# One matmul for V's mean row, one normalisation per head, and third-product operands made a quarter earlier

## The chip, the cores and the metric

The kernel runs on one core of a Trainium2 chip. The metric is the device time of one execution in microseconds (us); a lower time is better. Names of engines as the profile has them: PE is the matrix engine (PEld its weight loads), DVE the vector engine, ACT the scalar engine, POOL the GpSimd engine, SP the engine that issues most DMA transfers (SPq is its queue of issues).

## What is computed

Three stages follow each other, all in fp32 at the interface:

```python
mask   = q_bucket[:, :, :, None] == k_bucket[:, :, None, :]   # 6 sign bits of q@proj, k@proj
scores = np.where(mask, q @ k.T / 8, -1e9)                    # B=2, H=8, S=768, D=64
attn   = softmax(scores) @ v                                  # 16 heads
x = attn -> (1536, 512)
h = max(x @ w1, x @ w2, x @ w3)                               # 512 -> 768
x = h @ w_out                                                 # 768 -> 512, "the third product"
h = x @ w_in                                                  # 512 -> 2048
out = (h * clip(h + 3, 0, 6) / 6) @ w_out2                    # 2048 -> 512
```

A query that shares its bucket with no key gets -1e9 everywhere, so its softmax is uniform and its output is the mean of V's rows.

## The kernel before

Precision is kept by splitting: an fp32 operand is written as a high part and a residual, and a product becomes three matmuls (high x high, high x residual, residual x high). The two large products after the third one are computed by a seven-product scheme on 2x2 blocks, whose operands are blocks (B11, B21, B22) and differences of blocks (T1 to T4), each split in two.

**Attention** (`attention()`, L357) is one list of 96 steps, s = (head h, half hf, block i). The order of work is written out by hand: functions are put on steps by `at` (before the steps' end) and `po` (the `late` tasks), with the offsets of tables such as `VA, VS, VC, VH` counted from a pair's first step s0 = 12p. The loop at the end of `attention()` issues, for each step s: the PV block of step s - LAG (LAG = 6); the tasks called `first` (the normalisation, and from step RAMP = 8 on every task whose name isn't in AFTER); the scores of step s; the row maxima of a later head (`max_unit`); the split of the exponentials of step s - 1; the remaining tasks; the late tasks; and pieces of weight preparation (`tick`). The engines' queues run in this order, each its own.

What the functions put on the engines:

- `scores` (L659 ff.): PE, four matmuls of 384 columns (L664) into two PSUM tiles "s"; ACT then takes the exponential (L668, tile E) and its fp16 copy (L671, ph); POOL (L686) or DVE makes the residual pl.
- `max_unit` (L609): PE, two matmuls (L614) into PSUM tiles "m" (three exist), each read out by a DVE maximum (L618).
- `pv` (L689): PE, 18 fp16 matmuls of 65 columns (L698 to L700) into the PSUM tile "x", of which there is one, and two matmuls (L703, L704) that add V's mean row to flagged queries. Their weights are the flag row FL (zero but in row 0), their moving operand is VM, whose row 0 holds the mean's high part and then its residual.
- `norm` (L706): DVE reads x: denominator (L710, xd), reciprocal (L715, xr), product (L718, xo), three blocks at a time, so twice per head.
- `fin` (L723): PE transposes xo (L726).
- `vsum` (L541): PE, one matmul with one column (L543) that reduces V's row maxima into an "m" tile; `vscale` (L545) is four small DVE steps on it (L549, L554 and on).
- `vmean` (L590): V's mean. `max_out` (L646): SP issues the transfers of the maxima's rows and of FL (L651).

**The third product** runs in four quarters (b, dh) = (0,0), (0,1), (1,1), (1,0), each with two column tiles d and six steps f of six matmuls (L1453). After each f the loop advances the generator `making` by MK = 0, 3, 3 or 2 steps (one step is one instruction) and prepares weights (`tick2`, by the table TQ). `making` is `xops` (L1150): for each block an optional subtraction on DVE (L1161, xF), the high part on ACT (L1164, xh) and the residual on DVE (L1166, xl) or POOL. At a quarter's end ACT evicts the PSUM tiles into xF (L1481). In the fourth quarter `seven` (L1197) begins between the f steps: its first product (L1210) is copied by ACT into c (L1216), and further products, c matmuls of L1210, are added on it. Weight preparation uses the names wy, wr, wh, wl, G (ACT L954, L956, L1015; DVE L961; POOL L984).

The lines of the third product's loop:

```python
for _ in range(MK[3 * b + dh - 2 * b * dh]):
    next(making, None)
tick2(TQ[3 * b + dh - 2 * b * dh][d % 2][f])
...
if (b, dh) == (0, 1):
    for _ in making:
        pass
    making = xops(0, [(free.pop(0), free.pop(0)) for _ in range(7)], XO[0])
```

The functions that the diff touches, and those that call them:

## Time and profile before

| | |
|---|---|
| median of 3 runs | 688.95 us (688.47 to 689.98) |
| the profiled execution's own time | 690.18 us |
| its span (first to last instruction) | 688.4 us |
| mean granted TensorE clock | 0.993 of 2.4 GHz |
| PE busy | 666.0 us, 97% of the span |
| DVE, ACT, POOL busy | 511.0, 432.8, 334.3 us |

The profile is of one execution; the times are of others, of the same program. A busy time is the sum over instructions; an idle time is given with the releaser, the instruction whose end allowed the engine to go on. Attention takes about the first 250 us, the first products of the next stage follow, the third product lies at about 373 to 438 us, and the large products fill the rest.

### The profile page before, as it was taken

Reading aid. Unit: us, or ns where it says so; the run is one execution under the profiler, and the core shown is the slowest. Engines: PE = TensorE matmul, PEld = TensorE weight load, DVE = VectorE, ACT = ScalarE, POOL = GpSimd, SP = SyncE. Lnnn points to the kernel's source line nnn. Section 1 sums busy time; section 2 is a strip of 40 time slices with the busy share of each in tenths; the row PEclk is TensorE's granted clock in tenths of the full one; section 3 lists DMA queues with packets and bytes.
Section 4 is the critical chain, followed back from the end, with each engine's and each line's share of the span. In section 5 each row is a group of like instructions: output and inputs, shape, how many; then the busy total and the mean of one; then the engine's idle time right before and its main releaser. Section 6 shows DMA issues by size and latency. Waiting matters only on the chain.

```text
span 688.4 us, 13482 instructions
## 1 busy us (share of the span) xinstructions
PE 666.0 (97%) x5189; PEld 613.2 (89%) x5189; DVE 511.0 (74%) x978; ACT 432.8 (63%) x749; POOL 334.3 (49%) x280
## 2 busy tenths in 40 slices
PE   8999999999999999999999996999999999999997
PEld 7789898888898989999999996989989889889986
DVE  6888988989985647677668477773868687877664
ACT  6667788889887525574746556676556565655520
POOL 6778898999987330654443543112142331313100
PEclk9999999999999999999999998999999999999999
DMA  6665557767441000211223222010203020211004
GB/s 191 170 153 136 160 123 184 191 167 190 103 90 63 2 1 32 92 62 62 62 92 120 96 64 89 31 62 1 92 30 123 31 92 31 92 61 62 1 0 184
DMA packets 22527, 61.80 MB, mean 90 GB/s; under 512 B 3864, under 2 KB 4952, under 8 KB 22464
## 3 DMA queue, kind: packets, MB, share of 16 engines
q1 hardware_dynamic: 22032, 60.55, 30.7%
q8 instruction: 41, 0.67, 0.4%
q10 hardware_dynamic: 432, 0.40, 0.2%
q14 instruction: 22, 0.18, 0.1%
HBM read 38.87 MB, written 3.15 MB: 61 GB/s over the span
## 4 chain that ended last, share of the span: by engine, by line
PE 63%; DVE 6%; ACT 2%; issue 1%; POOLq 0%; DVEq 0%; ACTq 0%
PE c L1210 16%; PE m L1210 11%; PE x L1536 10%; PE m L1536 9%; PE c L147 4%; PE m L307 3%; PE m L1453 2%; PE s L664 2%; PE c L1453 2%; PE x L1210 1%; DVE xF L1161 1%; PE x L698 1%; PE x L699 1%; PE x L700 1%; DVE mx L618 1%
## 5 line engine op out<-in xcount | busy, mean ns | idle before, releaser
L686 POOL TENSOR_TENSOR pl<-E,ph 128x768 f16<-128x768 f32 x85 | 152.4, 1808 | 30.4 <-ACT ph L671 17.2
L618 DVE TENSOR_REDUCE mx<-m 128x1 f32<-128x384 f32 x192 | 96.6, 546 | 12.3 <-PE m L614 11.4
L668 ACT ACTIVATE E<-s 128x768 f32<-128x768 f32 x96 | 78.1, 813 | 39.1 <-PE s L664 31.4
L671 ACT ACTIVATE ph<-s 128x768 f16<-128x768 f32 x85 | 68.9, 810 | 0.0
L698 PEld LDWEIGHTS <-ph 128*128 128x128 f16 x576 | 53.9, 98 | 16.3 <-issue 10.2
L698 PE MATMUL x<-VV,ph 128*128 128x65 f16 x576 | 64.5, 195 | 2.8 <-DVE xo L718 1.9
L699 PE MATMUL x<-VV,ph 128*128 128x65 f16 x576 | 64.1, 196 | 0.0
L700 PE MATMUL x<-VV,pl 128*128 128x65 f16 x576 | 63.7, 193 | 0.0
L614 PE MATMUL m<-T,T 76*128 76x384 f32 x192 | 54.0, 352 | 3.5 <-DVE mx L618 1.5
L664 PE MATMUL s<-QB,KB 128*128 128x384 f32 x192 | 56.7, 376 | 0.4 <-ACT ph L671 0.4
L699 PEld LDWEIGHTS <-ph 128*128 128x128 f16 x576 | 54.5, 98 | 0.7 <-issue 0.6
L700 PEld LDWEIGHTS <-pl 128*128 128x128 f16 x576 | 54.7, 99 | 0.0
L664 PE MATMUL s<-T,T 98*128 98x384 f32 x192 | 49.7, 340 | 0.3 <-DMA T<-mr 0.2
L1006 POOL TENSOR_TENSOR hF<-hF 128x256 f32<-128x256 f32 x8 | 6.6, 819 | 76.6 <-DVE hF L965 76.6
L614 PEld LDWEIGHTS m<-T,T 76*128 76x128 f32 x192 | 35.0, 188 | 9.6 <-DVE mx L618 5.7
L961 DVE SCALAR_TENSOR_TENSOR wy<-wy,wr 128x512 int32<-128x512 int32 x32 | 23.0, 718 | 25.9 <-ACT wr L956 25.9
L1554 DVE TENSOR_TENSOR xF<-x,xF 128x512 f32<-128x512 f32 (+1 forms) x43 | 29.4, 684 | 11.6 <-PE x L1536 11.5
L984 POOL TENSOR_TENSOR wl<-wy,wh 128x512 fp32r<-128x512 f32 x10 | 13.2, 1323 | 50.8 <-ACT wh L982 50.8
L1094 POOL TENSOR_TENSOR hF<-hF 128x256 f32<-128x256 f32 x6 | 6.5, 1090 | 62.7 <-DVE hF L1048 62.7
L664 PEld LDWEIGHTS s<-T,T 98*128 98x128 f32 x192 | 34.9, 189 | 0.9 <-DMA T<-mr 0.9
L984 POOL TENSOR_TENSOR wol<-wy,woh 128x512 fp32r<-128x512 f32 x6 | 8.0, 1342 | 51.6 <-ACT woh L982 51.6
L1252 ACT ACTIVATE gr<-m,half 128x384 f32<-128x384 f32 x30 | 17.4, 579 | 24.1 <-DVE m L1230 13.5
(472 smaller groups left out, 2198.2 us busy)
## 6 DMA issues: line engine op xcount, KB each, us to landing
wraw<-in_wts_dram SPq DMA_DIRECT2D x56, 512.0 KB
xF<-in_vP_dram SPq DMA_DIRECT2D x8, 384.0 KB
KB<-kH SPq DMA_DIRECT2D x15, 192.0 KB
QB<-qL SPq DMA_DIRECT2D x15, 192.0 KB
T<-kH SPq DMA_DIRECT2D x15, 192.0 KB
T<-qH SPq DMA_DIRECT2D x15, 192.0 KB
KB<-kL SPq DMA_DIRECT2D x15, 192.0 KB
QB<-qH SPq DMA_DIRECT2D x15, 192.0 KB
```

The lines of the kernel that those rows point to most:

```text
L614: pe.matmul(u[:, 0:HF], QA[h % NA][0:76, qt * 128:qt * 128 + 128], KA[h % NA][0:76, hsl(hf)], start=True, stop=True,)
L618: dve.tensor_reduce(out=mx[h][:, qt, hf:hf + 1], in_=u[:, 0:HF], axis=AX.X, op=ALU.max)
L664: pe.matmul(u[:, k, 0:HF], a[0:n, c], b[0:n, hsl(hf)], start=n == 128, stop=n < 128)
L668: act.activation(out=e, in_=u[:, :, 0:HF], func=AF.Exp, scale=BIG)
L671: act.activation(out=ph.rearrange("p (a b) -> p a b", a=2), in_=u[:, :, 0:HF], func=AF.Exp, scale=BIG,)
L686: eng.tensor_tensor(out=pl, in0=e, in1=ph, op=ALU.subtract)
L698: pe.matmul(o, ph[:, c], vv[:, 0:65], start=kt == 0, stop=False)
L699: pe.matmul(o, ph[:, c], vv[:, 65:130], start=False, stop=False)
L700: pe.matmul(o, pl[:, c], vv[:, 0:65], start=False, stop=False)
L1210: pe.matmul(u, l[:, s], r[i], start=first and i + j == 0, stop=i == 1 and j == 2, skip_group_check=not first,)
L1536: pe.matmul(u[:, 0:c1 - c0], (h, l, h)[k], (oh, oh, ol)[k][:, c0:c1], start=j == k == 0, stop=j == 1 and k == 2,)
L1554: dve.tensor_tensor(out=o, in0=u[:, 0:c1 - c0], in1=o, op=ALU.add)
```

## The change

- V's mean: `VM` is now one row of 65 columns per head, with the high part in row 0 and the residual in row 32 (of a tile that is cleared otherwise); the flag row is sent to rows 0 and 32 of FL, and one matmul adds both.
- All six PV blocks of a head go into one "x" tile, and `norm` is called once per head, on six blocks. Since there is one such tile, the first PV block of the next head is issued behind the scores and maxima of its step instead of ahead of them.
- V's scale matmul and the four DVE steps behind it move a step later (VS, VC), and with `vsum` gone from AFTER the matmul is issued ahead of the step's scores.
- The third product's first two split operands (B11, T1) are made in quarter (0,1) instead of (1,1), and the second half of quarter (1,1) has three weight ticks fewer (TQ).

```diff
--- before.py
+++ after.py
@@ -31,7 +31,7 @@
 WS = (4, 0, 4, 2, 2, 2)
 LAG = 6
 RAMP = 8
-AFTER = ("vmean", "vsum")
+AFTER = ("vmean",)
 WARM = (9, 4, 3, 1)
 TAIL = 88
 TKF = (1, 1, 1)
@@ -55,14 +55,14 @@
 BT = (-13, -13)
 BO = (-12, -11)
 AL = (-9, -6)
-VA, VS, VC, VH, VL, VE = -9, -6, (-6, -6, -6, -2), -2, -1, 2
+VA, VS, VC, VH, VL, VE = -9, -5, (-5, -5, -5, -2), -2, -1, 2
 MF, MO = -3, -2
 FN = (29, 32)
 XE1 = (1, 1, 1, 1)
 XS = 0
 WL = (1, 0, 0, 0, 0)
 WH = 2
-TQ = (((2, 1, 2, 1, 2, 1), (2, 1, 2, 1, 2, 1)), ((1, 1, 1, 1, 1, 2), (1, 1, 1, 1, 1, 1)), ((1, 1, 1, 1, 1, 1), (1, 1, 1, 1, 1, 1)), ((1, 1, 1, 1, 0, 1), (1, 0, 2, 1, 1, 1)))
+TQ = (((2, 1, 2, 1, 2, 1), (2, 1, 2, 1, 2, 1)), ((1, 1, 1, 1, 1, 2), (1, 1, 1, 1, 1, 1)), ((1, 1, 1, 1, 1, 1), (1, 0, 1, 0, 1, 0)), ((1, 1, 1, 1, 0, 1), (1, 0, 2, 1, 1, 1)))
 TS = 0
 IS = 2
 PR = (3, 4)
@@ -91,7 +91,7 @@
 NW = 8
 PJ = 4
 LAGO = 1
-XO = ((0, 1, 2, 3, 4, 5, 6),)
+XO = ((0, 1), (2, 3, 4, 5, 6))
 TN = (0, 1, 1)
 OG = (1, 1, 1, 1)
 PSB = (("s", 2, 2), ("x", 1, 1), ("m", 3, 1))
@@ -361,7 +361,7 @@
         a3 = es.enter_context(tc.tile_pool(name="a3", bufs=3))
         ag = es.enter_context(tc.tile_pool(name="ag", bufs=LAG + 2))
         VV = [ap.tile([128, KT, 2, VW], F16, name=f"VV{i}") for i in range(2)]
-        VM = [ap.tile([128, 2, VW], F16, name=f"VM{i}") for i in range(2)]
+        VM = [ap.tile([128, 2, 65], F16, name=f"VM{i}") for i in range(2)]
         FL = [ap.tile([128, S], F16, name=f"FL{i}") for i in range(3)]
         up = ap.tile([128, NP], F32, name="up")
         KB, QB = {}, {}
@@ -597,12 +597,12 @@
                         o, one16, w[:, kt, :, c:c + 65], start=kt + c == 0,
                         stop=kt == KT - 1 and c > 0,
                     )
-            m = ap.tile([1, 2, 64], F32, name="vm_m")
-            act.activation(out=m, in_=o[0:1, :, 0:64], func=AF.Copy, scale=1.0 / S)
-            vm = VM[p % 2][0:1]
+            m = ap.tile([33, 2, 64], F32, name="vm_m")
+            act.activation(out=m, in_=o[0:33, :, 0:64], func=AF.Copy, scale=1.0 / S)
+            vm = VM[p % 2][0:33, :, 0:64]
             eng = pool if p else dve
-            eng.tensor_copy(out=vm[:, :, 0:64], in_=m)
-            eng.tensor_tensor(out=vm[:, :, 65:129], in0=m, in1=vm[:, :, 0:64], op=ALU.subtract)
+            eng.tensor_copy(out=vm, in_=m)
+            eng.tensor_tensor(out=vm[32:33], in0=m[32:33], in1=vm[32:33], op=ALU.subtract)
 
         mx = {}
 
@@ -648,7 +648,8 @@
             c = slice(0, S) if q is None else hsl(q)
             for i in range(2):
                 copy(QA[h % NA][96 + i:97 + i, c], r[:, i, :], eng)
-            (eng or sp).dma_start(out=FL[h % 3][0:1, c], in_=g)
+            for r in (0, 32):
+                (eng or sp).dma_start(out=FL[h % 3][r:r + 1, c], in_=g)
 
         def ph_dve(s):
             return s % 6 in PH_TAIL if s >= TAIL else s in PH_HEAD if s < 12 else s % 12 in PH_DVE
@@ -688,9 +689,9 @@
 
         def pv(h, hf, q):
             p, j = divmod(h, 2)
-            if q == 0:
-                st["X", h, hf] = unit("x")
-            o = st["X", h, hf][:, 66 * q:66 * q + 65]
+            if hf == q == 0:
+                st["X", h] = unit("x")
+            o = st["X", h][:, 66 * (3 * hf + q):66 * (3 * hf + q) + 65]
             for kt in range(KT):
                 ph, pl = st["P", h, hf, kt // 2]
                 c = slice(HF * (kt % 2) + 128 * q, HF * (kt % 2) + 128 * q + 128)
@@ -699,25 +700,23 @@
                 pe.matmul(o, ph[:, c], vv[:, 65:130], start=False, stop=False)
                 pe.matmul(o, pl[:, c], vv[:, 0:65], start=False, stop=False)
             c = slice(hf * HF + 128 * q, hf * HF + 128 * q + 128)
-            f, vm = FL[h % 3][:, c], VM[p % 2][:, j, :]
-            pe.matmul(o, f, vm[:, 0:65], start=False, stop=False)
-            pe.matmul(o, f, vm[:, 65:130], start=False, stop=True)
-
-        def norm(h, hf):
+            pe.matmul(o, FL[h % 3][:, c], VM[p % 2][:, j, :], start=False, stop=True)
+
+        def norm(h):
             p, j = divmod(h, 2)
-            X = st.pop(("X", h, hf))[:, 0:198].rearrange("p (b d) -> p b d", b=3)
-            d = a2.tile([128, 3], F32, name="xd")
+            X = st.pop(("X", h))[:, 0:396].rearrange("p (b d) -> p b d", b=6)
+            d = a2.tile([128, 6], F32, name="xd")
             dve.tensor_scalar(
                 out=d, in0=X[:, :, 64], scalar1=1e-9, scalar2=up[:, p:p + 1],
                 op0=ALU.add, op1=ALU.mult,
             )
-            r = a2.tile([128, 3], F32, name="xr")
+            r = a2.tile([128, 6], F32, name="xr")
             dve.reciprocal(out=r, in_=d)
-            if j == 0 and hf == 0:
+            if j == 0:
                 st["xo", p] = a2.tile([128, 6, 128], F32, name="xo")
             dve.tensor_tensor(
-                out=st["xo", p][:, 3 * hf:3 * hf + 3, 64 * j:64 * j + 64], in0=X[:, :, 0:64],
-                in1=r.unsqueeze(2).to_broadcast([128, 3, 64]), op=ALU.mult,
+                out=st["xo", p][:, :, 64 * j:64 * j + 64], in0=X[:, :, 0:64],
+                in1=r.unsqueeze(2).to_broadcast([128, 6, 64]), op=ALU.mult,
             )
 
         def fin(p, hf):
@@ -826,8 +825,7 @@
                 if h:
                     at(s0 + 6 * j + MF, max_fin, h)
                     at(s0 + 6 * j + MO, max_out, h)
-                for hf in range(2):
-                    at(s0 + 6 * j + 3 * hf + 2 + LAG, norm, h, hf)
+                at(s0 + 6 * j + 5 + LAG, norm, h)
             for hf in range(2):
                 at(s0 + FN[hf] if p < NP - 1 else s0 + 15 + LAG + 3 * hf, fin, p, hf)
         for k, s in enumerate(XH):
@@ -854,7 +852,8 @@
 
         prologue()
         for s in range(NST + LAG):
-            if 0 <= s - LAG < NST:
+            after = (s - LAG) % 6 == 0 and 0 <= s < NST
+            if 0 <= s - LAG < NST and not after:
                 pv(*idx(s - LAG))
             todo = tasks.pop(s, [])
             first = [t for t in todo if t[0] is norm]
@@ -867,6 +866,8 @@
             gs = [max_unit(m // 6, m % 6) for m in mu.get(s, ())]
             for g in gs:
                 next(g, None)
+            if after and s >= LAG:
+                pv(*idx(s - LAG))
             if 0 <= s - 1 < NST:
                 psplit(*idx(s - 1), gs)
             for g in gs:
@@ -1480,6 +1481,8 @@
                 for hf in range(2):
                     act.activation(out=X[:, 4 * b + d, hsl(hf)], in_=us[hf][:, 0:HF], func=AF.Copy)
             if (b, dh) == (0, 0):
+                xo = [(free.pop(0), free.pop(0)) for _ in range(7)]
+                making = xops(0, xo, XO[0])
                 while ("w", 23) not in held2:
                     tick2()
                 h2 = slots.pop(0)
@@ -1491,7 +1494,7 @@
             if (b, dh) == (0, 1):
                 for _ in making:
                     pass
-                making = xops(0, [(free.pop(0), free.pop(0)) for _ in range(7)], XO[0])
+                making = xops(0, xo, XO[1])
                 free += own[0]
                 a, b_ = ((free.pop(0), free.pop(0)) for _ in range(2))
                 pslots.append({
```

On PE, at the end of a head: x is the PV result, FL the flags, VM the mean row, s the scores, m the maxima or scratch; L726 and L725 are the same transposes. Before:

```order
L703 LDWEIGHTS FL_139
L703 MATMUL x<-VM_135,FL_139 128x65
L704 LDWEIGHTS FL_139
L704 MATMUL x<-VM_135,FL_139 128x65
L726 MATMUL m<-ident,xo 128x128 x3
L664 MATMUL s<-QB,KB 128x384 x2
L664 MATMUL s<-T_92,T_87 128x384 x2
L614 MATMUL m<-T_89,T_94 128x384 x2
L698 LDWEIGHTS ph
```

and of the changed kernel at the same place:

```order
L703 LDWEIGHTS FL_139
L703 MATMUL x<-VM_135,FL_139 128x65
L725 MATMUL m<-ident,xo 128x128 x3
L665 MATMUL s<-QB,KB 128x384 x2
L665 MATMUL s<-T_92,T_87 128x384 x2
L614 MATMUL m<-T_89,T_94 128x384 x2
L665 MATMUL s<-QB,KB 128x384 x2
L665 MATMUL s<-T_93,T_88 128x384 x2
L614 MATMUL m<-T_89,T_94 128x384 x2
L699 LDWEIGHTS ph
```

One flag matmul is gone, and a second step's scores and maxima now stand ahead of the next head's first PV block.

On PE, V's scale matmul L543, before:

```order
L664 MATMUL s<-QB,KB 128x384 x2
L664 MATMUL s<-T_93,T_88 128x384 x2
L614 MATMUL m<-T_89,T_94 128x384 x2
L543 MATMUL m<-vs_s,ones 128x1
L698 LDWEIGHTS ph
```

and of the changed kernel:

```order
L703 MATMUL x<-VM_136,FL_137 128x65
L543 MATMUL m<-vs_s,ones 128x1
L665 MATMUL s<-QB,KB 128x384 x2
L665 MATMUL s<-T_93,T_88 128x384 x2
L614 MATMUL m<-T_89,T_94 128x384 x2
```

It stood behind a step's maxima; now a whole PV block stands between the maxima and it, and the scores are queued behind it.

On ACT, in the second and third output quarter (L1481 evicts, L1164 makes high parts of the operands, L1015 those of weights, L954 and L956 begin a weight). Before:

```order
L1481 ACTIVATE xF<-c 128x384 x2
L954 ACTIVATE wy<-wraw 128x512
L956 ACTIVATE wr<-wraw 128x512
L1481 ACTIVATE xF<-m 128x384
L1481 ACTIVATE xF<-x 128x384
L1164 ACTIVATE xh_99<-xF 128x768
L1015 ACTIVATE G_5220<-hF_105 128x512
L1164 ACTIVATE xh_100<-xF 128x768
L1015 ACTIVATE G_5220<-hF_106 128x256
```

and of the changed kernel, where the first two operands' high parts stand:

```order
L1482 ACTIVATE xF<-m 128x384 x2
L1165 ACTIVATE xh_99<-xF 128x768
L1016 ACTIVATE wh_113<-hF_105 128x512
L1165 ACTIVATE xh_100<-xF 128x768
L1016 ACTIVATE woh_5027<-hF_106 128x256
L1016 ACTIVATE wh_117<-hF_105 128x256
L1016 ACTIVATE wh_115<-hF_106 128x512
L1016 ACTIVATE woh_5027<-y_5059 128x256
L955 ACTIVATE wy<-wraw 128x512
L957 ACTIVATE wr<-wraw 128x512
L1482 ACTIVATE xF<-c 128x384 x2
```

The two high parts, which stood behind the second quarter's evictions, now stand a quarter earlier, ahead of its first half's evictions. PE's order after attention is the same in both kernels.

## Rows read from the trace of the kernel before

**Rows 1.** The page's part 1, busy us (share of the span) and instructions of each engine.

```profile
PE 666.0 (97%) x5189; PEld 613.2 (89%) x5189; DVE 511.0 (74%) x978; ACT 432.8 (63%) x749; POOL 334.3 (49%) x280
```

**Rows 2.** Windows, four periods of 12 steps: us, busy PE, PEld, DVE, ACT, POOL, PEclk, DMA, GB/s.

```profile
89.21:114.57 25.36, 25.34 (x347) 23.13 (x346) 21.89 (x55) 20.71 (x30) 22.30 (x15) 1.00 0.65 168
114.57:141.56 26.99, 26.21 (x348) 23.24 (x347) 26.21 (x62) 24.75 (x39) 24.05 (x16) 1.00 0.72 178
141.56:168.82 27.26, 26.36 (x346) 23.12 (x346) 25.12 (x61) 24.04 (x37) 25.46 (x17) 1.00 0.67 176
168.82:196.24 27.42, 25.98 (x346) 23.18 (x347) 25.31 (x60) 23.98 (x37) 25.83 (x17) 1.00 0.49 114
```

**Rows 3.** PE's timeline, flag matmuls: start us, us, instruction, [idle before, releaser].

```profile
202.56 0.19 PE L703 MATMUL x<-VM,FL 128*128 128x65 f16 x1
202.59 0.20 PE L704 MATMUL x<-VM,FL 128*128 128x65 f16 x1
202.62 0.27 PE L634 MATMUL m<-ident,mq 128*6 128x128 f32 x1
```

**Rows 4.** Groups by line on DVE: the normalisation. Busy us, mean ns | idle before.

```profile
L718 DVE TENSOR_TENSOR xo<-x,xr 128x192 f32<-128x192 f32 x32 | 11.4, 357 | 1.5
...
L710 DVE TENSOR_SCALAR xd<-x,up 128x3 f32<-128x3 f32 x32 | 6.7, 209 | 8.2 <-PE x L704 8.2
...
L715 DVE RECIPROCAL xr<-xd 128x3 f32<-128x3 f32 x32 | 5.6, 176 | 1.1
```

**Rows 5.** PE's timeline, two waits for DVE.

```profile
117.00 0.38 PE L543 MATMUL m<-vs_s,ones 128*128 128x1 f32 x2 [0.49 <-DVE mx L618]
...
242.24 0.20 PE L698 MATMUL x<-VV,ph 128*128 128x65 f16 x1 [1.48 <-DVE xo L718]
```

**Rows 6.** DVE's timeline, ahead of the scale's steps.

```profile
143.70 1.02 DVE L618 TENSOR_REDUCE mx<-m 128x1 f32<-128x384 f32 x2 [1.27 <-PE m L614]
```

**Rows 7.** SP's timeline, two issues of transfers.

```profile
25.94 0.66 SPq L651 DMA_DIRECT2D FL<-mf  x1
...
37.57 0.80 SPq L142 DMA_DIRECT2D QB<-qL  x1
```

**Rows 8.** ACT's timeline, opening.

```profile
41.63 0.84 ACT L442 ACTIVATE kH<-kr 128x768 fp32r<-128x768 f32 x1 [2.17 <-DMA QB<-qL]
```

**Rows 9.** The chain of waits, 398 to 440 us, in order of time: start us, us.

```profile
398.92 0.74 ACT xh L1164
...
403.99 1.43 DVE xF L1161
...
419.28 1.52 ACT xF L1481 x4
...
423.88 0.39 ACT c L1216
424.31 2.29 PE c L1210 x6
...
430.08 1.04 PE m L1453 x6
```

**Rows 10.** PE's timeline, within the fourth quarter.

```profile
424.31 1.01 PE L1210 MATMUL c<-G,wh 128*128 128x384 f32 x2 [5.33 <-ACT c L1216]
```

**Rows 11.** DVE's timeline, second quarter.

```profile
392.08 1.59 DVE L961 SCALAR_TENSOR_TENSOR wy<-wy,wr 128x512 int32<-128x512 int32 x1 [4.39 <-ACT wr L956]
```

**Rows 12.** Windows, two rests of PE (columns as in rows 2).

```profile
240.00:242.00 2.00, 0.77 (x5) 0.45 (x3) 1.93 (x6) 0.98 (x2) 1.79 (x1) 1.00 0.04 8
...
423.00:425.00 2.00, 0.69 (x2) 0.69 (x3) 2.00 (x2) 1.67 (x4) 0.66 (x1) 0.50 0.23 88
```

**Rows 13.** POOL's pl (L686): ns of one, least/median/most; from when to when.

```profile
L686 POOL TENSOR_TENSOR pl<-E,ph x85: 1631/1652/2558, 20.8 to 235.0; 128x768 f16<-128x768 f32 x85
```

**Rows 14.** The page's costliest groups, ACT's exponential and its copy.

```profile
L668 ACT ACTIVATE E<-s 128x768 f32<-128x768 f32 x96 | 78.1, 813 | 39.1 <-PE s L664 31.4
L671 ACT ACTIVATE ph<-s 128x768 f16<-128x768 f32 x85 | 68.9, 810 | 0.0
```

## The prediction

> **What bounds the kernel now.** I read the page's busy shares first: the matrix engine PE is busy 97% of the span [rows 1], so only two things can shorten the kernel, fewer PE instructions or fewer PE waits. Then I cut the attention stage into periods of 12 steps (one pair of heads each), from one PV block's first matmul to another's [rows 2]. Once weights are split beside attention, a period takes 26.99, 27.26 and 27.42 us, where the last one without that load takes 25.36, with the same PE work. The difference, 1.63 + 1.90 + 2.06 = 5.59 us, is waiting, and DVE with 25 to 26 us of busy time is what it waits for, with ACT and POOL at 24 to 26 close behind. After attention one place stands out in the chain of waits and in PE's timeline: half way through the fourth output quarter PE stands still for 5.33 us and then runs at half clock. So I cost attention and that place apart.
>
> **Flag matmuls.** The change takes one of the two matmuls on FL out of each of the 96 PV blocks. In PE's timeline the two start at 202.56 and 202.59 and the next instruction at 202.62 [rows 3]: 0.03 us each, weight load hidden. 96 x 0.03 = 2.9 us. Twelve blocks lie in the opening, where PE waits for others (below), so I take 84 x 0.03 = **2.5 us**. On the other engines this costs nothing: the copies for the mean row keep their width per partition and only use 33 partitions instead of one, and the memory that POOL clears halves, in the prologue.
>
> **Normalisation and the scale matmul.** Each of the 32 normalisations costs DVE 209 + 176 + 357 ns [rows 4]. Per period four (2.97 us) become two, whose last operation is twice as wide; no row has it, so it lies between 0.36 us (width free) and 0.71 us (width is everything). At 0.55 the two cost 1.87 us: DVE is relieved of 1.1 us a period (0.8 to 1.5). The normalisations that go are those in the middle of a head. At the head's end PE now issues a whole further step (scores, maxima) ahead of the next block, so it waits for DVE less there too.
>
> The scale matmul (L543) stands now behind the step's maxima and needs a PSUM tile that DVE must first empty: PE waited 0.49 us for it at 117.00 [rows 5], and at 144 DVE itself had stood idle 1.27 us for PE [rows 6], each waiting for the other. A step later, and ahead of the scores, the maxima of the last step are mostly read out, and its DVE users come behind other work. What is queued behind it on PE are the scores, so if DVE is late they are late by the same wait, once a period.
>
> So DVE gets back 1.1 us of work and about half of its own 1.27 us per loaded period. Bounds for the three together: nothing, if ACT or POOL (24 to 25.8 us of busy time) hold the pace, and 5.59 us, if all goes. I take 1.2 us of each period's waits, **3.6 us**, nearer to the upper end because DVE's row is the fullest in two of the four. For the quieter periods and the last full steps I add **0.5** (0 to 1.5).
>
> At 242.24 one PV block waits 1.48 us for a mid-head normalisation [rows 5], which stood in DVE's queue behind the splits of the next stage. That normalisation is gone, the tile goes on to be filled: **1.5 us** (0 if the one at the head's end waits instead; no more).
>
> **More transfers.** Each normal head now sends its flag row twice. An issue occupies SP for 0.66 us at 25.94 [rows 7], with 0.1 us to the next, and SP runs without a gap from there to the QB transfer issued at 37.57. Two additional issues lie in that stretch (the transfers at 25.94 and at 34.44), and the first one, at 17, has a gap behind it. ACT waited 2.17 us for that QB transfer, until 41.63, before it could overwrite kH [rows 8], with the next exponentials queued behind it and PE waiting for those. So I charge 2 x 0.75 = **1.5 us lost**. Bounds: nothing, if the transfers, not their issue, set the landing, and 3 us, if PE's longer wait also costs clock. The Trainium skill, "DMA: Bandwidth & Descriptors", section on the anatomy of one DMA, puts a sequencer's dispatch at about 50 ns; by that the loss would be an estimated 0.1 us and the total 1.4 us better, but the row shows 0.66, and I keep the row. Later SP has idle stretches, and I charge nothing.
>
> **The third product.** Here "making" turns seven blocks into split operands in the third quarter. The chain of waits [rows 9] starts at 398.92 with the first, goes to and fro between ACT and DVE, and only then lets ACT evict the third quarter's results (419.28) and copy c (423.88), for which PE has waited 5.33 us [rows 10]. The change makes the first two operands a quarter earlier. They fill 398.92 to 403.99 of that chain, 5.07 us; the third operand's subtraction needs only blocks that are evicted by 398.9. Before that, DVE has idle time for them (4.39 us before 392.08 [rows 11]). No PE instruction moves. So c comes at about 419.2 instead of 424.27, while PE arrives at 424.31 - 5.33 = 418.98: a wait of 0.2 to 0.3. The three weight ticks left out of this quarter can only shorten ACT's queue; the weights they advance are late by at most some steps and are used far later.
>
> The clock adds to it. After the stop the granted clock was 0.50 from 423 to 425 [rows 12], the 1.2 GHz level; the first six matmuls took 2.29 us, those at 430.08 1.04 us. From 424.31 to 430.08 PE ran 18, which would take 3.12: 2.65 us lost. At 240 to 242 PE was idle over half the time and the clock stayed at 1.00 [rows 12], so a rest of some tenths should not lower it. 5.33 + 2.65 = 7.98; I leave 0.6 for the rest of the wait: **7.4 us** (1.7 to 8.0).
>
> **Sum.** 2.5 + 3.6 + 0.5 + 1.5 - 1.5 + 7.4 = 14.0 us. The profiled execution took 690.18 (span 688.4), which gives 676.2. It stands 1.2 us above the median of the runs, 688.95, so I forecast **675.0**.
>
> **Rivals.**
> A: *another engine takes over in attention.* ACT and POOL are within two or three us of a period's length [rows 2], so DVE's relief may only uncover them. Against it: part of POOL's busy time is itself lengthened, as its pl takes 1.63 to 2.56 us [rows 13]. Then attention's loaded periods gain 0.5 in all, the flags show half (1.2), and the sum is 1.2 + 0.5 + 1.5 - 1.5 + 7.4 = 9.1: about 680.
>
> B: *the operands made earlier get in the way.* In the second quarter the three moved DVE operations meet POOL's weight differences, whose results ACT must split before it evicts. pl's spread [rows 13] shows what such meetings do to POOL. If POOL loses the whole 3.6 us that those operations take at most (the 5.07 less two ACT operations of 0.74 [rows 9]), the third operand starts that much later, PE still waits 5.33 - (5.07 - 3.6) = 3.9 us, and the clock may fall as before: the third product then gives 1.5, or 4.1 with the clock kept. Total 8.1 to 10.7: 678 to 681. The Trainium skill, "SBUF — State Buffer", section on the two separate sides, states the rule behind such meetings: a DVE operation with two SBUF inputs and a POOL operation that reads SBUF exclude one another for a whole instruction. The trace agrees in kind (1.63 against 2.56); but in this stretch POOL has idle time, and its results are needed late, so I think it mostly harmless.
>
> C, slower: *two steps of scores in a row.* Once per head PE now issues a second set of scores at most 1.5 us after the first (25.36 / 12 = 2.1 for a step, less its PV block of 20 x 0.03), into two PSUM tiles, and ACT needs 0.81 + 0.81 us per set [rows 14]. If ACT is late by one full pair (1.6 us) at each of the 15 head boundaries, PE loses 24 us against 14 gained: 699. It decides from 14 / 15 = 0.9 us late at every boundary on. Against it: ACT's own waiting is for PE's scores, 31.4 us [rows 14], so it is normally early.
>
> That the flag row's second half would not be summed is excluded: both rows lie in the one matmul's contraction.
>
> **Chances.** Forecast (third product gives over 5, attention over 4 net), 671 to 678: 0.62. A 0.17 and B 0.14, 678 to 682; both together would be near 685 and lie within these. More than forecast, with all waits gone and no loss in the opening (2.9 + 5.6 + 1.5 + 1.5 + 8.0 = 19.5): 669.5: 0.04. C and other losses: 0.03. The range **669.5 to 682.5** leaves out C, both together and a little at the ends, under 2 in 10. A measurement of this kernel tells 0.2% (1.4 us) from no change; faster by more 0.96, within it 0.02, slower 0.02.
>
> **What would show it.** PE's 5.33 us stop before line 1211's c matmuls should be under 1 us, with the granted clock at 1.00 from 415 on; if it is over 3, B holds. The three loaded periods should take 25.5 to 26.3 us each; over 26.8 with POOL or ACT filled is A. The wait of 1.48 us near the end of attention should be gone, ACT's wait for QB near 41 should be 3 to 4 us instead of 2.17, and 96 matmuls fewer should stand in PE's list. Waits of PE for the exponentials at head boundaries above 0.9 us would be C, and prove me wrong.

## The result, and the profile after

| | before | after |
|---|---|---|
| median | 688.71 us (688.18 to 689.98, 4 runs) | 682.46 us (682.27 to 683.91, 4 runs) |
| ratio, 95% interval | | 0.9911 (0.9892 to 0.9931) |
| profiled execution, span | 690.18, 688.4 us | 682.4, 680.6 us |

The kernel is 0.9% faster, 6.2 us by the medians; I had forecast 14. Where the 7.8 us between the two profiled executions lie is quickly said: at one and the same transposition near the end of attention (L726, L725 after) PE is at 250.99 before and 251.12 after, so attention as a whole gave nothing, and all of it comes behind. Within attention two things cancel. The second PV block of the third head starts at 65.83 before and 67.00 after, so the opening became 1.17 us longer. From there to the last transpositions it takes 1.03 us less, where the prediction's terms for that stretch add up to about 8. The windows, of before, then of after (us, PE, PEld, DVE, ACT, POOL, PEclk, DMA, GB/s):

```profile
65.83:258.13 192.30, 187.26 (x2445) 169.73 (x2444) 156.10 (x367) 146.89 (x214) 152.73 (x95) 1.00 0.46 117
```

```profile
67.00:258.27 191.27, 185.89 (x2367) 167.38 (x2364) 153.33 (x324) 146.00 (x214) 152.45 (x95) 1.00 0.46 118
```

PE is busy 1.37 us less there, where 83 flag matmuls of 0.03 us are 2.5; its idle time, which the other edits aimed at, is 5.04 us before and 5.38 after.

Page part 1 of after, to be read beside [rows 1]:

```profile
PE 661.3 (97%) x5093; PEld 607.8 (89%) x5093; DVE 508.3 (75%) x930; ACT 431.5 (63%) x749; POOL 337.6 (50%) x280
```

96 matmuls and 48 DVE instructions fewer, as planned. PE's timeline of after within the fourth quarter, to be read beside [rows 10], and the windows around it, beside [rows 12] (columns as above):

```profile
418.77 0.34 PE L1454 MATMUL c<-T,wol 128*128 128x384 f32 x1
419.22 0.62 PE L1211 MATMUL c<-G,wh 128*128 128x384 f32 x2
```

```profile
419.00:421.00 2.00, 1.90 (x11) 1.78 (x11) 1.79 (x4) 1.03 (x3) 0.00 (x0) 1.00 0.02 8
421.00:423.00 2.00, 2.00 (x14) 2.00 (x13) 1.23 (x4) 2.00 (x6) 1.29 (x1) 1.00 0.64 190
```

The matmuls on c start 0.45 us after the start of the one before them instead of 5.66, and the granted clock stays at 1.00 (2.4 GHz) where it had been at 0.50. That is the third product's term; third_only below gives its size.

For attention I cut the periods here at the second block of a head, since the first one has moved. Windows of before, then of after (columns as above):

```profile
91.11:117.25 26.14, 25.63 (x350) 23.10 (x349) 23.42 (x58) 21.73 (x32) 22.64 (x15) 1.00 0.64 166
117.25:144.55 27.30, 26.43 (x348) 23.17 (x348) 25.28 (x61) 25.06 (x39) 25.22 (x17) 1.00 0.75 184
144.55:171.48 26.93, 26.13 (x349) 23.19 (x348) 25.14 (x61) 23.71 (x36) 25.13 (x17) 1.00 0.66 176
171.48:198.14 26.66, 25.70 (x348) 23.21 (x348) 24.70 (x60) 22.98 (x35) 25.07 (x16) 1.00 0.47 109
```

```profile
92.08:117.77 25.69, 25.34 (x341) 22.82 (x338) 21.64 (x50) 21.08 (x31) 22.27 (x15) 1.00 0.65 167
117.77:144.88 27.11, 25.75 (x340) 22.73 (x337) 25.15 (x56) 24.55 (x38) 24.97 (x16) 1.00 0.72 182
144.88:171.55 26.67, 25.76 (x341) 22.77 (x337) 24.76 (x55) 24.24 (x38) 25.11 (x17) 1.00 0.68 180
171.55:199.65 28.10, 26.52 (x340) 22.88 (x337) 26.21 (x55) 23.43 (x36) 25.27 (x17) 1.00 0.47 107
```

Together 107.03 before and 107.57 after, though DVE has fewer instructions in each. The first three are shorter by 0.45, 0.19 and 0.26, about a period's flag matmuls (0.36); the last is longer by 1.44. PE's waits from 60 to 252 us (what waited, for what: us, times, longest), of before and of after:

```profile
PE x L698 <- DVE xo L718: 1.9, 3, 1.5
PE m L543 <- DVE mx L618: 1.4, 3, 0.5
PE m L614 <- DVE bt L513: 0.8, 1, 0.8
```

```profile
PE s L665 <- DMA T<-mr: 1.7, 3, 0.9
PE m L614 <- DVE bt L513: 1.0, 1, 1.0
PE m L614 <- DVE wy L220: 0.7, 2, 0.4
PE m L614 <- DVE mf L643: 0.6, 2, 0.4
PE m L307 <- DVE hF L314: 0.5, 1, 0.5
PE m L614 <- DVE mx L618: 0.5, 2, 0.3
```

Both waits that the change aimed at are gone (normalisation, scale matmul: 3.3 us), and 4.0 us of others stand there: at a head's first scores PE waits for the row maxima's transfer, at the maxima for DVE's weight steps. DVE itself now idles more ahead of its maxima (16.9 us instead of 12.3 by its groups): it was relieved, and nobody used it.

The long last period has one clear cause in the trace. The two timelines there, before and after:

```profile
185.36 1.01 DVE L585 SCALAR_TENSOR_TENSOR VV<-xF,up,VV 128x768 f16<-128x768 f32 x1
...
185.44 2.44 POOL L686 TENSOR_TENSOR pl<-E,ph 128x768 f16<-128x768 f32 x1
```

```profile
186.01 1.64 POOL L687 TENSOR_TENSOR pl<-E,ph 128x768 f16<-128x768 f32 x1
...
186.15 2.33 DVE L585 SCALAR_TENSOR_TENSOR VV<-xF,up,VV 128x768 f16<-128x768 f32 x1
```

Before, DVE's residual of V started 0.08 us ahead of POOL's subtraction, took 1.01, and POOL was stretched to 2.44 instead of 1.65. After, POOL was 0.14 us ahead, and DVE took 2.33, with the maxima queued behind it. The Trainium skill, "SBUF — State Buffer", section on the two separate sides, says that of such a pair the one that starts first keeps the shared port for its whole instruction; these four numbers agree to within 0.2 us (0.93 to DVE's end plus 1.65 against POOL's 2.44; 1.50 to POOL's end plus 1.01 against DVE's 2.33). I had cited that rule for the third product, where it did no harm; it struck here.

### The profile page after: what moved, and what is told of

It is laid out like the page before. It is cut to its first block, busy times and chain, and to the rows that moved or that the text cites. A ratio compares the mean times of both kernels' runs of the same rounds, so it can differ in the third digit from the quotient of the medians.

```text
span 680.6 us, 13308 instructions
## 1 busy us (share of the span) xinstructions
PE 661.3 (97%) x5093; PEld 607.8 (89%) x5093; DVE 508.3 (75%) x930; ACT 431.5 (63%) x749; POOL 337.6 (50%) x280
## 4 chain that ended last, share of the span: by engine, by line
PE 63%; DVE 6%; ACT 2%; issue 1%; POOLq 0%; DVEq 0%; ACTq 0%
PE c L1211 16%; PE m L1211 11%; PE x L1539 10%; PE m L1539 9%; PE c L147 4%; PE m L307 3%; PE m L1454 2%; PE s L665 2%; PE c L1454 2%; DVE xF L284 1%; PE x L1211 1%; DVE xF L1162 1%; PE m L614 1%; PE x L700 1%; PE x L699 1%
## 5 line engine op out<-in xcount | busy, mean ns | idle before, releaser
L618 DVE TENSOR_REDUCE mx<-m 128x1 f32<-128x384 f32 x192 | 96.9, 547 | 16.9 <-PE m L614 16.2
L669 ACT ACTIVATE E<-s 128x768 f32<-128x768 f32 x96 | 78.2, 815 | 39.6 <-PE s L665 33.8
L699 PE MATMUL x<-VV,ph 128*128 128x65 f16 x576 | 63.2, 195 | 0.0
L700 PE MATMUL x<-VV,ph 128*128 128x65 f16 x576 | 62.8, 195 | 0.0
L614 PE MATMUL m<-T,T 76*128 76x384 f32 x192 | 56.6, 359 | 5.5 <-DVE mx L618 2.0
L1557 DVE TENSOR_TENSOR xF<-m,xF 128x512 f32<-128x512 f32 (+1 forms) x42 | 28.5, 679 | 4.6 <-PE m L1539 4.6
```

Source lines behind the costliest of these rows:

```text
L614: pe.matmul(u[:, 0:HF], QA[h % NA][0:76, qt * 128:qt * 128 + 128], KA[h % NA][0:76, hsl(hf)], start=True, stop=True,)
L618: dve.tensor_reduce(out=mx[h][:, qt, hf:hf + 1], in_=u[:, 0:HF], axis=AX.X, op=ALU.max)
L669: act.activation(out=e, in_=u[:, :, 0:HF], func=AF.Exp, scale=BIG)
L699: pe.matmul(o, ph[:, c], vv[:, 0:65], start=kt == 0, stop=False)
L700: pe.matmul(o, ph[:, c], vv[:, 65:130], start=False, stop=False)
L1557: dve.tensor_tensor(out=o, in0=u[:, 0:c1 - c0], in1=o, op=ALU.add)
```

## The experiments

Each was timed beside the kernel before on the same chip. Ratios are to the kernel before, with their interval.

### Which part gives the gain: attn_only, third_only

`attn_only` is the changed kernel with this taken back, `third_only` the kernel before with only this (shortened; the TQ row is that of the third quarter's second half):

```diff
-TQ third quarter: (1, 1, 1, 1, 1, 1)
+TQ third quarter: (1, 0, 1, 0, 1, 0)
-XO = ((0, 1, 2, 3, 4, 5, 6),)
+XO = ((0, 1), (2, 3, 4, 5, 6))
+making = xops(0, xo, XO[0])      # after quarter (0, 0)
```

> The changed kernel with the third product as it was: only the three edits to attention remain. By the prediction they give 2.5 + 3.6 + 0.5 + 1.5 - 1.5 = 6.6 us, so about 682. By the theory formed on the two traces (the whole gain of the change comes from the third product, and in attention new waits take back what the edits give) the time is that of the kernel before within 1 us, ratio 0.998 to 1.002. Rival A of the prediction gives about 1.7 us.

> The kernel before with only the third product's edit (two operands a quarter earlier, three weight ticks left out). By the prediction 7.4 us less, ratio 0.9893; by the theory on the traces 7.5 us less, so as fast as the whole change within 1 us. Rival B gives 1.5 to 4.1 us less. PE's wait of 5.33 us half way through the fourth quarter should be gone and the granted clock 1.00 from 415 on.

**attn_only 1.0027 (1.0009 to 1.0045), third_only 0.9896 (0.9868 to 0.9924).** The third product's edit alone is as fast as the whole change; its segment behind attention is 7.63 us shorter in the profile, 7.66 in that of the whole change. third_only makes two edits at once, and no run separates the earlier operands from the three weight ticks left out; that the operands did it is read from the chain, of which they had filled 5.07 us and in which the matmuls on c now come 5.22 us earlier, counted from the transposition named above. The three attention edits together came out 0.27% slower than the kernel before. Part of that is the clock: the twelve runs of attn_only have a mean granted clock of 0.988 against 0.992 of those of the kernel before, by an estimate 0.004 x 690 = 2.8 us, so what the edits cost or give without it stays open. In attn_only's profile PE waited 1.4 us for the row maxima near 145, and right after it the clock fell to its lower level:

```profile
144.00:146.00 2.00, 0.94 (x9) 0.81 (x10) 0.79 (x3) 1.18 (x3) 2.00 (x2) 1.00 0.60 135
146.00:148.00 2.00, 2.00 (x40) 2.00 (x37) 1.55 (x4) 1.89 (x3) 1.84 (x3) 0.50 0.98 204
```

### The flag edit and its transfers: flags_only, flagdma_only

The edits, shortened:

```diff
+            for r in (0, 32):
+                dma_start(out=FL[h % 3][r:r + 1, c], in_=g)   # both kernels
-            pe.matmul(o, f, vm[:, 0:65], ...)                 # flags_only
-            pe.matmul(o, f, vm[:, 65:130], ...)
+            pe.matmul(o, FL[h % 3][:, c], VM[p % 2][:, j, :], ...)
```

> The kernel before with only the flag edit: one matmul per PV block for V's mean row, the flag row sent twice. By the prediction 2.5 us less for 84 matmuls and 1.5 us more in the opening: 1.0 us less, ratio 0.9985. If the second transfer costs more than priced (the changed kernel's first head boundary shows PE waiting 2.10 us for the row maxima), it is the same or slower. If sending twice costs nothing, 2.5 to 2.9 us less, 0.996.

> The kernel before, with the flag row sent twice and nothing else (row 32 of FL meets zeros in VM). It prices the transfers alone. By the prediction 1.5 us more (ratio 1.002), all of it before 60 us; if an issue at about 50 ns were the price, 0.1 us; if the landing of later transfers counts too, 2 to 3 us (1.003 to 1.004). After 60 us no difference.

**flags_only 0.9996 (0.9974 to 1.0018), flagdma_only 1.0025 (1.0002 to 1.0048).** The second transfer alone costs 0.25%, 1.7 us, near the price I had given (1.5), with an interval from 0.1 to 3.3 us. The Trainium skill, "DMA: Bandwidth & Descriptors", section on the anatomy of one DMA, has some 50 ns for a sequencer's dispatch. That section is about transfers issued by GpSimd; carried over to SP's queue, as I did in the prediction, it gives an estimated 0.1 us. What decides is not this run, whose interval begins there, but SP's row below: 1.43 us for the two issues. Part of the 1.7 us may be clock, which fell twice in the opening of flagdma_only's profile (28 to 34 and 48 to 54 us) and once in before's (46 to 52). In flagdma_only's profile the two kernels run alike behind 66 us (no period differs by over 0.34); ahead of that PE waited for the row maxima (page of waits, 16 to 60 us):

```profile
PE s L665 <- DMA T<-mr: 1.1, 1, 1.1
```

The changed kernel shows the same place: SP's double issue, and PE waiting 2.10 us at 38.38 (timelines):

```profile
36.62 1.43 SPq L652 DMA_DIRECT2D FL<-mf  x2
```

```profile
38.38 0.58 PE L665 MATMUL s<-T,T 98*128 98x384 f32 x2 [2.10 <-DMA T<-mr]
```

In flags_only the stretch from the block at 59.38 to 254.67 is 1.47 us shorter than before's from 54.23 to 250.99, where 89 matmuls of 0.03 are 2.7. Most of the difference went into waits for the normalisation, which PE now reaches earlier: 2.8 us in six instead of 1.9 in three.

```profile
PE x L699 <- DVE xo L717: 2.8, 6, 1.6
```

### The normalisation edit and the scale matmul: norm_only, pvafter_only, scale_only

norm_only is the edit of the diff (one tile, one `norm(h)`, the first PV block behind the scores). pvafter_only is only its last part:

```diff
+            after = (s - LAG) % 6 == 0 and 0 <= s < NST
-            if 0 <= s - LAG < NST:
+            if 0 <= s - LAG < NST and not after:
                 pv(*idx(s - LAG))
...
+            if after and s >= LAG:
+                pv(*idx(s - LAG))
```

scale_only sets VS and VC from -6 to -5 and takes vsum out of AFTER.

> The kernel before with only the normalisation edit: one tile and one normalisation per head, the next head's first PV block behind its step's scores and maxima. By the prediction it carries most of 3.6 + 0.5 + 1.5 us: 4 us less, ratio 0.994. By the theory on the traces PE then comes about 0.6 us earlier to each head's scores and waits there for the transfer of the row maxima (up to 0.89 us at one boundary): 0 to 1.5 us less, 0.998 to 1.000.

> The kernel before with only the move of a head's first PV block behind its step's scores and maxima; the two normalisations per head stay, and no work is removed. By the prediction it costs nothing or gains a little (PE waits less for the normalisation). By the theory after the runs it makes the wait for the row maxima's transfer, some 1 to 1.5 us between 91 and 171, and meets the late residual (L585 2.3 us in the period that norm_only and the changed kernel lengthened by 1.45): up to 60 us no loss, after it 1 to 2.5 us more, ratio 1.001 to 1.004.

> The kernel before with only V's scale matmul and its DVE steps a step later. By the prediction PE's waits at L543 (1.4 us in all) and half of DVE's own idle 1.27 us in three periods go: 0.7 to 1.5 us less, 0.998 to 0.999. By the theory after the runs PE waits at the next maxima for the weights' DVE steps instead (0.4 to 0.6 us in two periods): 0 to 0.7 us less.

**norm_only 0.9997 (0.9978 to 1.0016), pvafter_only 0.9969 (0.9955 to 0.9983), scale_only 1.0007 (0.9993 to 1.0020).** Here my theory after the first runs fell too: I thought that moving the PV block was what cost, and it gains 0.3%. norm_only has the merge of the normalisations on top, which takes 1.1 us of DVE's work out of every period, and that gain is gone. Not all of it is the merge. Of the 3.0 us between the two profiles at the end of attention, 2.25 lie ahead of the third head's second PV block (66.09 and 63.84), where norm_only's clock fell twice (18 to 24 and 30 to 34 us) and pvafter_only's stayed at 1.00; behind it the merge costs 0.72 us, and there the move by itself gives 1.32 against before. In norm_only the period at 170.89 has the long residual (2.34 us) and is 1.45 longer than before; in pvafter_only, with the block moved as well, the residual takes 1.01 and the period is 0.37 longer. Moving the scale matmul renames the wait, and the time stays the same; PE's waits of scale_only, 60 to 252 us:

```profile
PE x L698 <- DVE xo L718: 2.9, 6, 1.5
PE m L614 <- DVE wy L220: 1.5, 3, 0.5
PE m L614 <- DVE bt L513: 0.8, 1, 0.8
```

### The new waits one by one: after_again, mr_earlier, vlo_later, raw_behind

```diff
-MF, MO = -3, -2           # mr_earlier: maxima finished and sent a step earlier
+MF, MO = -4, -3
-VH, VL, VE = -2, -1, 2    # vlo_later: V's residual a step later
+VH, VL, VE = -2, 0, 2
-JS = 38                   # raw_behind: weights a step later, behind the maxima
+JS = 39
```

> The changed kernel itself, beside its variants: ratio 0.991 to 0.9925. By both theories PE waits some 1.5 us in all for the row maxima's transfer at head boundaries between 60 and 250 us, and the residual of V (L585) of the fifth pair's period takes about 2.3 us instead of 1.0 to 1.4.

> The changed kernel with the row maxima of a head finished and sent one step earlier (MF, MO = -4, -3). If the wait for that transfer at the head boundaries is what takes back the gain of the normalisation edit, PE's waits for it go and the time falls by 1.4 to 2 us against the changed kernel. Rival: PE then waits for DVE ahead of the transposition of the maxima (L634), or DVE falls behind elsewhere, and the time stays within 0.7 us.

> The changed kernel with the residual of V (L585) made one step later (VL = 0 instead of -1). If its 2.33 us in the period from 171.55 to 199.65 come from POOL having started a subtraction just ahead of it, then with another start it takes 1.0 to 1.4 us there, and the period is about 1.4 us shorter (26.7 instead of 28.1), the time 1 to 1.4 us less, unless it meets POOL in another period. Rival: the period is long because DVE has too much to do in it; then it stays above 27.5.

> The changed kernel with the preparation of weights beside attention started a step later (JS = 39), so that the 512 KB load of a weight is issued behind the row maxima's transfer of a head, not just ahead of it. If that load is what makes the row maxima land late, PE's waits for them at head boundaries between 91 and 200 us (1.0 to 1.7 us) go, and the time falls by 1 to 1.5 us against the changed kernel (0.9898): 0.988. Rival: the weights' own steps, a step later, meet other work of DVE and PE waits for those, as when the maxima were sent earlier: 0.990 or more.

**after_again 0.9898 (0.9874 to 0.9922), mr_earlier 1.0217 (1.0187 to 1.0247), vlo_later 0.9881 (0.9852 to 0.9909), raw_behind 0.9963 (0.9947 to 0.9980).** Two of the three mended the wait they aimed at and lost elsewhere. With the maxima sent earlier PE no longer waited for them behind 60 us, but SP now issued a head's flags, KB and QB ahead of the weight's load, and the lateness went on from engine to engine, load to ACT to DVE to PE (waits of mr_earlier, 60 to 210 us):

```profile
PE m L614 <- DVE wy L220: 11.1, 3, 3.9
DVE m L217 <- ACT wr L204: 10.8, 3, 4.1
ACT m L193 <- DMA wraw<-in_wts_dram: 9.5, 3, 3.5
```

With the weight's load behind the maxima there is no wait for the maxima left either behind 60 us, which fits the load as what made them late (the weight's steps on ACT and DVE moved with it). But PE's waits became those below (raw_behind, 60 to 252 us; this profile is of the slowest of its twelve runs, 689.88 against a median of 685.98):

```profile
PE m L614 <- DMA KB<-kL: 2.4, 1, 2.4
PE m L614 <- DVE mx L618: 2.2, 4, 0.7
PE m L614 <- DVE wy L220: 1.7, 3, 0.6
```

vlo_later took the last period from 28.08 (after_again) to 27.14, as expected, with the residual at 1.22 there. But in the other periods it met POOL each time (median 1.93 us instead of 1.16), and between its ratio and that of after_again the intervals leave the gain unclear.

### With the opening mended: third_flags_late, all_late, pv_flags_late, norm_flags_late, pv_flags_late_raw, norm_late_vlo_early

The flag rows of all but the first half head are sent some steps later, that of the first head behind the opening's transfers:

```diff
+            if q == 0:
+                flag_out(h, c, g)
+            else:
+                at(6 if h == 0 else 6 * h + 2, flag_out, h, c, g)
```

third_flags_late has this, the flag edit and the third product's. pv_flags_late adds the moved PV block, norm_flags_late the merged normalisation on top, pv_flags_late_raw adds JS = 39 to pv_flags_late, all_late is the changed kernel with late flags and VL = 0.

> The kernel before with the third product's edit and the flag edit, and with the flag rows of each head (except the first half of the first) sent some steps later, behind the transfers of the opening. If the transfers alone ate the flag edit's gain (flagdma_only cost 0.25%), the opening is no longer than before and the loaded and quiet steps gain some 1.5 us: ratio 0.987 to 0.988, against 0.9896 of the third product alone. Rival: PE then comes earlier to the normalisations and waits there for DVE, or PV waits for the flags: 0.9896 or more.

> The changed kernel with V's residual a step later (as in vlo_later, 0.9881) and the flag rows sent later (as in third_flags_late). If the two losses are separate, 1.5 us less than vlo_later: ratio 0.986, about 680. Rival: the opening waits for something else (the row maxima's transfer at the first head's end stays), and it is 0.988.

> Third product's edit, flag edit with the flag rows sent later, and a head's first PV block behind its step's scores; the two normalisations per head as before. If the parts add up (0.9868 for the first two, 0.9969 for the third), 0.984, about 678. If the move of the PV block gained only by an opening in which the clock happened to stay up, 0.9868.

> As pv_flags_late, and the two normalisations merged to one per head, which is all that differs: DVE has about 1.1 us less to do in each period. By the prediction that relief is worth some 0.7 us in each loaded period and 1.5 us at the end of attention: 3 us less than pv_flags_late. By the theory after the runs (DVE's total does not bound the loaded periods, only what stands in its queue at single places) it is worth nothing there, gains 1 us at the end and loses about 1 us where V's residual meets POOL: within 1 us of pv_flags_late, or slower.

> pv_flags_late with the weights' preparation a step later too (JS = 39). By the same theory PE's waits for the row maxima, about 1 us after 60 us, go: 0.7 to 1 us less than pv_flags_late. Rival as for raw_behind: no gain, or a loss.

**third_flags_late 0.9868 (0.9846 to 0.9891), all_late 0.9909 (0.9881 to 0.9936), pv_flags_late 0.9869 (0.9848 to 0.9890), norm_flags_late 0.9904 (0.9882 to 0.9925), pv_flags_late_raw 0.9925 (0.9898 to 0.9952).** third_flags_late, 679.82 us, came out as expected and has the lowest median of all kernels, with pv_flags_late (679.97) beside it. Against the changed kernel (0.9898 to 0.9911) it is 2.1 to 3.0 us better, though its interval overlaps that of after_again.

The moved PV block's 0.3% does not add to it, and 0.9869 is the figure that I had put down for the case that its gain came from an opening in which the clock happened to stay up. The profiles bear this out in part: behind the third head's second block the move gives 0.7 us here (190.76 against 191.44), and the opening, where pv_flags_late's clock fell twice and third_flags_late's not, is 3.1 us longer. So a gain of the move is seen behind the opening, 0.7 to 1.3 us, and not shown in the kernel's time. all_late met neither its expectation (0.986) nor its rival (0.988), and why stays open; in its profile the clock fell once more, from 184 to 188 us. pv_flags_late_raw lost, as its rival had it.

norm_flags_late and pv_flags_late differ by the merge alone: 0.35%, 2.3 us slower with less work on DVE, though the two intervals overlap a little. The profiled executions take about as long (681.35 and 681.66 us), because pv_flags_late's opening is 2.2 us longer at a lower clock. From the third head's second block to the end of attention norm_flags_late takes 1.85 us more, and so the merge lost behind the opening in both pairs, by 0.72 us (norm_only against pvafter_only) and by 1.85 us. Windows of norm_flags_late, of pv_flags_late:

```profile
64.51:257.12 192.61, 185.73 (x2360) 166.86 (x2360) 153.34 (x324) 145.87 (x213) 151.44 (x95) 1.00 0.45 116
```

```profile
66.74:257.50 190.76, 184.15 (x2361) 167.28 (x2361) 156.56 (x366) 146.05 (x213) 151.92 (x95) 1.00 0.45 117
```

DVE is busy 3.2 us less with the merge, and the stretch is longer. The period that differs (windows of norm_flags_late, of pv_flags_late):

```profile
169.85:198.85 29.00, 26.67 (x337) 22.98 (x337) 26.74 (x55) 24.75 (x37) 24.89 (x17) 1.00 0.44 104
```

```profile
171.47:198.51 27.04, 25.68 (x336) 22.81 (x336) 25.75 (x60) 23.80 (x36) 25.99 (x17) 1.00 0.47 111
```

Five DVE instructions fewer, 0.99 us more of DVE's busy time, and 1.96 us more in all; the residual takes 2.34 there with the merge and 1.01 without. The last run moved it, with the merge kept (shortened):

```diff
-VC, VH, VL = (-6, -6, -6, -2), -2, -1
+VC, VH, VL = (-6, -6, -6, -3), -3, -2
```

> norm_flags_late with V's high part and residual (L568, L585) made one step earlier (VC, VH, VL one less), so that the residual no longer stands right behind the merged normalisation in DVE's queue. If the merge loses because the residual, 0.2 us later than before, now starts behind POOL's subtraction and takes 2.34 us, it takes 1.0 to 1.4 us again in that period, the period from 169.85 to 198.85 falls from 29.0 to about 27.3, and the time by 1 to 1.7 us: 0.988. Rival: the residual meets POOL in other periods, or the merged normalisation itself holds PE at the head's end: the period stays above 28.3 and the time within 0.7 us.

**1.0056 (1.0035 to 1.0077).** The residual takes 1.27 us in every period (median of seven), and the period in question fell from 29.00 to 27.62, close to what the theory said. But the four loaded or quiet periods ahead of it grew by 1.4 to 2.9 us each: ACT's high part of V, one step earlier, stands ahead of ACT's exponentials and waits for DVE's scale (waits of ACT, 60 to 262 us, of norm_flags_late and of this run). At the end of the longest of them the clock fell as well, to 0.50 from 150 to 152 us.

```profile
ACT VV L568 <- DVE up L562: 2.4, 6, 0.5
```

```profile
ACT VV L568 <- DVE up L562: 9.2, 6, 2.3
```

So the residual's meeting with POOL is the greater part of that period's loss (1.38 of 1.96 us), by a run that changed other waits as well; what the rest is stays open.

## Why the prediction was right or wrong

- **Third product, 7.4 us: right.** Measured 7.63 to 7.66 in the profiles, from the end of attention to PE's last matmul. The chain's start moved by what the two operands filled, PE's first matmul on c came at 419.22 where I had said that c comes at about 419.2, and with a rest of 0.11 us (418.77 + 0.34 to 419.22) the clock stayed up. Rival B did not happen: the moved operations met POOL in the second quarter and no one waited for it.
- **Opening, 1.5 us lost: borne out as far as the noise tells.** flagdma_only measured 1.7 (0.1 to 3.3), and the changed kernel's opening is 1.17 longer in the profile. What I had wrong was the first to wait: PE, for the row maxima's transfer, 2.10 us, and behind it ACT (2.69 instead of 2.17, now for the KB transfer; I had said 3 to 4). The granted clock fell in the opening of most of the profiles (in before's from 46 to 52 us), not in the same place, and in after's not at all, so one profile tells this part less well than twelve runs do.
- **Flag matmuls, 2.5 us: the mechanism right, a little over half the size.** The six plain blocks from 54 to 66 us are 0.19 us shorter, 0.03 each. Over all it was 1.47: I counted PE's time per block and left out that an earlier PE waits longer for the normalisation.
- **DVE's relief, 3.6 us in the loaded periods: wrong, and the step that failed.** I had taken a sum of waits (5.59 us) and the fullest engine's busy time, and concluded that less work on DVE shortens the waits. Both were misread. By [rows 2] PE's idle time in the three periods is 0.78 + 0.90 + 1.44 = 3.12 us, the rest of the 5.59 is longer PE busy time, and PE's list of waits has 2.5 us for DVE in them, less than the 3.6 that I took; and DVE's row is the fullest in one of the four periods, not in two. What came of it is nothing: behind the opening the changed kernel's attention takes 191.27 us, flags_only's 190.97, so the merge, the move and the scale matmul together took back 0.3 of what the flag matmuls gave, although the end of attention gained. The term's bound "nothing, if ACT or POOL hold the pace" came true in the time, but not by that cause: ACT and POOL were no fuller than before (146.00 and 152.45 us instead of 146.89 and 152.73 behind the opening). The waits belong to single places in the queues: each edit took its own wait away (1.9 and 1.4 us) and uncovered the next, PE at the maxima's transfer behind a 512 KB load, at the maxima behind DVE's weight steps, and a residual that now starts behind POOL's subtraction. That the relief by itself is worth nothing is shown by norm_flags_late beside pv_flags_late; which of the new waits costs how much is shown only for the residual, and in part. The width of the merged operation I had right: 0.558 us, forecast 0.55.
- **The end of attention, 1.5 us: two thirds.** The wait of 1.48 is gone; 0.54 for the next stage's split came in its place, and the segment is 1.0 us shorter (in norm_only 0.98).
- **Rival C: not seen.** ACT waits for PE's scores as before (33.8 us, 31.4 before). Behind 60 us PE waits for ACT's exponentials in none of the profiles of the changed kernel and its parts. In the opening there is one such wait, 0.35 us before and 0.81 after; flags_only, without two steps of scores in a row, has 1.7 us there, so the flags' transfers suffice for it. norm_late_vlo_early alone has one behind 60 us, 1.2.
- By their single runs the edits sum to -1.04 (third product) - 0.04 (flags) - 0.03 (normalisation) + 0.07 (scale matmul) = -1.04%; the whole change measured -0.89 and -1.02%. Of my sum only the third product was left, and the measured 682.46 us lies inside the range only at its upper end.

## What to carry to other kernels

Where several engines are each nearly full, don't price an engine's relief by the sum of the waits: name for each wait what stands ahead in which queue, and what PE would wait for next if it came earlier, and count the gain only up to there. A single stop behind which nothing else is late, like the 5.33 us here, can be priced from one chain, here to within 0.3 us. Split an edit that removes work from the move that comes with it: here, behind the opening, the move gained 0.7 to 1.3 us and the removal lost 0.7 to 1.9, by two pairs of single profiles. And compare stretches of profiles before totals: the opening varied by up to 7 us between these kernels, in part with its clock.

## What was not expected of the hardware

- Of two operations on DVE and POOL that meet, a lead of 0.1 us decides which one pays: 1.01 and 2.44 us with DVE first, 2.33 and 1.64 with POOL first, and in these two traces only DVE's delay reaches PE.
- In attn_only a PE wait of 1.4 us in the midst of attention was followed by 0.50 of the clock from 146 to 148 and 0.64 to 150; waits of up to 0.89 at head boundaries of after were not. The length of the wait alone does not decide: after the 2.10 us ahead of 38.38 in the changed kernel's opening the clock stayed at 1.00 (windows of after: us, PE, PEld, DVE, ACT, POOL, PEclk, DMA, GB/s).

```profile
36.00:38.00 2.00, 0.28 (x2) 0.00 (x0) 1.47 (x4) 0.73 (x2) 1.27 (x2) 1.00 0.28 96
38.00:40.00 2.00, 1.62 (x31) 1.49 (x32) 0.83 (x2) 0.94 (x2) 0.45 (x1) 1.00 0.47 75
```
